# Attention earlier in a unit, k and v of two heads in one transfer, and part of the q loads on SyncE's queue

## The chip, the cores and the metric

The kernel runs on one core of one Trainium2 chip. The metric is the device time in microseconds (us) of one execution, the median over several runs. TensorE multiplies matrices, VectorE and ScalarE do element-wise work, and three queues issue the DMA transfers: those of SyncE (SP in the profile), of GpSimd (POOL) and, at the start and the end, of ScalarE (ACT).

## The reference

Linear attention per head, a normalisation, and then a feed-forward layer with a squared ReLU:

```python
# q, k, v: (8 batches, 8 heads, 576 positions, 64)   all fp32
kv  = np.einsum('bhsd,bhse->bhde', k, v)         # one 64x64 matrix per batch and head
out = np.einsum('bhsd,bhde->bhse', q, kv)
rms = np.sqrt(np.mean(out * out, axis=-1, keepdims=True) + 1e-06)
x   = (out / rms * g_norm)                       # then (b,h,s,d) -> (b*s, h*d) = (4608, 512)
h = x @ w_in                                     # (4608, 2048)
r = np.maximum(h, 0.0)
g = s * (r * r) + b
y = g @ w_out                                    # (4608, 512)
```

## The kernel before

The 4608 rows are cut into nine units (u = 0 to 8) of 512 rows. A unit's first product (x @ w_in) has four steps, s = 0 to 3, and each step seven partial products (x1, z2, x6, y7, x5, x3, y4) of a Strassen-like scheme, so that VectorE and ScalarE add pieces between them. A unit's second product (g @ w_out) has the same seven partial products, and in units 2 to 8 the scheme is applied twice. While TensorE works on unit u, the attention for unit u + 1 is computed in two pairs of 128-row chunks, A and B, whose steps are hung into slots between the partial products.

Each engine works through its instructions in the order in which the program lists them, so the slot decides what stands ahead of what. The slots of the first product:

```python
        for s in range(NS if u > 0 else 0):
            a = steps[s]
            at(0)                       # runs first[(s, 0)]
            a["x1"]()
            if s:
                x3(steps[s - 1])        # product 3 of the step before, and its VectorE work
            a["z2"]()
            at(1)
            if s:
                y4(steps[s - 1])
            a["x6"]()
            at(2)
            a["y7"]()
            if s == NS - 1 and u > 1:
                second["sums"]()        # four sums for the second product
            at(3)
            a["x5"]()
```

What fills them, in unit 2 and in units 3 to 7:

```python
        kv = [lambda: kv_product(kv_due[u]), lambda: pump(NP)] if u in kv_due else []
        q = {half: [partial(loads, u + 2, half)] for half in range(2)}
        ...
        if u == 2:
            first = {
                (0, 2): [A["turn"]],
                (1, 1): kv,
                (1, 3): [A["product"]],
                (2, 0): [A["back"]],
                (2, 1): [A["square"]],
                (2, 2): [A["row_sum"], B["turn"]],
                (2, 3): [B["product"]],
                (3, 0): [B["back"]],
                (3, 1): [A["norm"]],
                (3, 2): [A["turn_x"], *q[0]],
                (3, 3): [B["square"]],
            }
            second = {
                0: [A["scale"]], 3: [B["row_sum"]], "norm": [B["norm"]],
                4: [B["turn_x"], B["scale"], *q[1]],
            }
        else:
            first = {
                (0, 2): [A["turn"]],
                (0, 3): [A["product"]],
                (1, 0): [A["back"]],
                (1, 1): [A["square"], *kv],
                (1, 2): [A["row_sum"]],
                (1, 3): [B["turn"]],
                (2, 0): [A["norm"]],
                (2, 1): [B["product"], *q[0]],
                (2, 2): [A["turn_x"], B["back"]],
                (2, 3): [B["square"]],
                (3, 0): [A["scale"], B["row_sum"]],
                (3, 1): [B["norm"]],
                (3, 2): [B["turn_x"], *q[1]],
            }
            second = {0: [B["scale"]]}
```

The steps: `turn` transposes q (VectorE), `product` multiplies it by kv (TensorE), `back` transposes the result (VectorE), `square` and `scale` are ScalarE's, `row_sum`, `norm` and `turn_x` VectorE's.

The loads. k and v of a batch come in four pairs of heads, one pair to a tile of a ring of seven, which the pieces of w_out share. `pump(k)` issues the next k ring loads on SyncE:

```python
    def load_kv_into(t, b, n):
        kv_in[b, n] = t.rearrange("p (m j d) -> p m j d", m=2, j=R)
        for m, src in enumerate((k, v)):
            for r in range(2):
                nc.sync.dma_start(
                    out=kv_in[b, n][r * HB : r * HB + HB, m],      # 64 partitions
                    in_=src[b, NP * r + n].rearrange("(p j) d -> p j d", j=R),
                )
```

q of a pair of chunks comes in 16 or 32 small loads on GpSimd (`load_q`, where `rest` is issued by `nc.gpsimd.dma_start`). In unit 1 the second product has 14 slots, numbered 0 to 13; `pump(2)` stands in the slots 1, 3, ... 13, and these are hung in after a slot's own work:

```python
                5: [A["row_sum"], B["turn"]],
                6: [A["norm"], partial(loads, 3, 0)],     # q of unit 3, first pair
                7: [A["turn_x"], A["scale"], B["product"], B["back"], B["square"]],
                8: [B["row_sum"]],
                9: [B["norm"], partial(loads, 3, 1)],     # q of unit 3, second pair
                11: [B["turn_x"], B["scale"]],
                12: [sums],
```

In unit 1 the pieces of w_out for the twice-applied scheme are also made, by VectorE, and stored to DRAM by GpSimd, once each for the products 1, 2, 6, 7, 3 and 4. A ring tile that holds such a piece is free only when its store has landed:

```python
        def parts_of_w(i):
            y = [[ring[u, i, n][:, :, q * P : q * P + P] for q in range(2)] for n in range(2)]
            (y11, y12), (y21, y22) = y
            ...                                           # t1 .. t4: four subtractions on VectorE
            for n, t in enumerate((y11, y21, t2, t3, t1, y22, t4)):
                nc.gpsimd.dma_start(out=w3_dram[i][:, n], in_=t)
```

The product of k and v works on 64x64 tiles of the array; r is the row half (one head each), l the head pair, and before the change l is also the column half:

```python
                for l in range(2):
                    for r in range(2):
                        rows = slice(r * HB, r * HB + HB)
                        nc.tensor.matmul(
                            ps[r][l * HB : l * HB + HB, i, :],
                            lhsT=kv[l][rows, 0, j, :],
                            rhs=kv[l][rows, 1, j, :],
                            start=(j == 0), stop=(j == R - 1),
                        )
```

Of the kernel before, what the change touches and what calls it, by code (L numbers as in the profile page):

```python
# [16 lines left out]
def kernel(  # L17
# [39 lines left out]
    nc = tc.nc  # L57
    P = 128
    B, H, S, D = q.shape
# [33 lines left out]

    kv_in, q_in, q_tile, w_raw = {}, {}, {}, {}

    def load_kv(b, i, pool, queues=(nc.sync, nc.sync), **kw):

        t = pool.tile([P, 4 * R * D], U32, name="kv_sb", **kw)
        view = t.bitcast(FP32).rearrange("p (m l j d) -> p m l j d", m=2, l=2, j=R)
        for l in range(2):  # L100
            kv_in[b, 2 * i + l] = view[:, :, l]
        for m, src in enumerate((k, v)):
            for r, queue in enumerate(queues):
                h = NP * r + 2 * i
                queue.dma_start(
                    out=view[r * HB : r * HB + HB, m].rearrange("p l j d -> p l (j d)"),
                    in_=src[b, h : h + 2].rearrange("h (p j) d -> p h (j d)", j=R),
                )

    def load_kv_into(t, b, n):  # L110

        kv_in[b, n] = t.rearrange("p (m j d) -> p m j d", m=2, j=R)
        for m, src in enumerate((k, v)):
            for r in range(2):
                nc.sync.dma_start(
                    out=kv_in[b, n][r * HB : r * HB + HB, m],
                    in_=src[b, NP * r + n].rearrange("(p j) d -> p j d", j=R),
                )

    def parts(c):  # L120

# [7 lines left out]
            return [(2 * g, 16, 2), (2 * g + 1, 0, 2)]  # L129
        return [(2 * g, 4 * i, 4)] if i < 4 else [(2 * g + 1, 4 * i - 18, 4)]  # L130

    def load_q(c, queues=(nc.sync, nc.sync)):

        t = qp.tile([P, 2 * DM], FP32, name="q_sb", tag="q")
        q_tile[c] = t
        pieces = []
        for i in range(2):
            if c + i < R:  # L140
                q_in[c + i] = t[:, i * DM : i * DM + DM].rearrange("p (h d) -> p h d", h=H)
        for s, queue in enumerate(queues):
            for i in range(2):
                if c + i < R:
                    b, j, _ = parts(c + i)[s]
                    queue.dma_start(
                        out=q_in[c + i][s * HB : s * HB + HB],
                        in_=q[b].rearrange("h (p j) d -> p j h d", j=R)[:, j],
                    )
        for i in range(2):  # L150
            if c + i < R:
                continue
            w = 4 * i
            for b, j, n in parts(c + i):
                if pieces and pieces[-1][1] == b and pieces[-1][2] + pieces[-1][3] == j:
                    pieces[-1][3] += n
                else:
                    pieces.append([w, b, j, n])
                w += n
            q_in[c + i] = t.rearrange("p (a w) -> p a w", a=NP)[:, :, i * P : i * P + P]  # L160
            if c + i == R:
                q_in[R] = t[:, DM:].rearrange("p (a w) -> p a w", a=NP)
        rest = []
        for w, b, j, n in pieces:
            src = q[b].rearrange("h (t j) d -> h t j d", j=JC)
            to = t.rearrange("p (a w d) -> p a w d", a=NP, d=32)
            if c < R:
                to, w = t[:, DM:].rearrange("p (a w d) -> p a w d", a=NP, d=32), 0
            for h in range(H):
                for a in range(2):  # L170
                    rows = slice(32 * (2 * (h % 2) + a), 32 * (2 * (h % 2) + a) + 32)
                    rest.append(
                        partial(
                            nc.gpsimd.dma_start,
                            out=to[rows, h // 2, w : w + n, :],
                            in_=src[h, :, j : j + n, a * 32 : a * 32 + 32],
                        )
                    )
        return rest
# [189 lines left out]
    def kv_product(b):  # L369


        ps = [ps_t.tile([P, 2, D], FP32, name="kv_ps", tag="t") for _ in range(2)]
        for i in range(2):
            if b == 0:
                warm((18, 7)[i])
            kv = [kv_in.pop((b, 2 * i + l)) for l in range(2)]
            for j in range(R):
                for l in range(2):
                    for r in range(2):
                        rows = slice(r * HB, r * HB + HB)  # L380
                        nc.tensor.matmul(
                            ps[r][l * HB : l * HB + HB, i, :],
                            lhsT=kv[l][rows, 0, j, :],
                            rhs=kv[l][rows, 1, j, :],
                            start=(j == 0),
                            stop=(j == R - 1),
                        )
        for r in range(2):
            for l in range(2):
                ls = slice(l * HB, l * HB + HB)  # L390
                to = bd_kv[b % 2][ls, 2 * r : 2 * r + 2, ls].rearrange("p i (c e) -> p i c e", c=KC)
                src = ps[r][ls].rearrange("p i (e c) -> p i c e", c=KC)
                if b == 0 and l == 1:
                    nc.vector.tensor_copy(out=to, in_=src)
                else:
                    nc.scalar.copy(to, src)
# [915 lines left out]
    def side_of(u):  # L1312

        A, B = pairs_of(u + 1)
        sums = lambda: [fn() for fn in x_sums(u + 1)]
        if u == 0:
            side = {
                6: [lambda: kv_product(1)],
                7: [partial(A["turn"], 0), partial(A["turn"], 1)],
                8: [A["product"], A["back"], A["square"]],  # L1320
                9: [A["row_sum"], partial(B["turn"], 0), partial(B["turn"], 1)],
                10: [A["norm"], A["turn_x"], A["scale"], B["product"], B["back"], B["square"]],
                11: [B["row_sum"], B["norm"]],
                12: [B["turn_x"], B["scale"], lambda: [fn() for fn in sums_w_in(0)]],
                13: [sums],
            }
        else:
            side = {
                2: [partial(A["turn"], 0), partial(A["turn"], 1)],
                4: [A["product"], A["back"], A["square"]],  # L1330
                5: [A["row_sum"], B["turn"]],
                6: [A["norm"], partial(loads, 3, 0)],
                7: [A["turn_x"], A["scale"], B["product"], B["back"], B["square"]],
                8: [B["row_sum"]],
                9: [B["norm"], partial(loads, 3, 1)],
                11: [B["turn_x"], B["scale"]],
                12: [sums],
            }
        return side

    def loads(u, i):

        if u < U:
            for load in load_q(4 * u + 2 * i):
                load()  # L1345

    tile_at = {1: 3, 2: 4, 3: 5, 4: 6, 5: 7, 6: 8, 7: 9, 9: 10, 10: 11, 11: 12, 12: 13, 14: 14, 15: 15}
    more_at = {8: 8, 9: 9, 12: 10, 13: 11, 14: 12, 15: 13}
# [19 lines left out]
    def sides(u):  # L1368
# [15 lines left out]
# [5 lines that stand above are left out]
                (2, 0): [A["back"]],  # L1389
                (2, 1): [A["square"]],  # L1390
                (2, 2): [A["row_sum"], B["turn"]],
                (2, 3): [B["product"]],
                (3, 0): [B["back"]],
                (3, 1): [A["norm"]],
                (3, 2): [A["turn_x"], *q[0]],
                (3, 3): [B["square"]],
            }
            second = {
                0: [A["scale"]], 3: [B["row_sum"]], "norm": [B["norm"]],
                4: [B["turn_x"], B["scale"], *q[1]],  # L1400
            }
        else:
            first = {
                (0, 2): [A["turn"]],
                (0, 3): [A["product"]],
                (1, 0): [A["back"]],
                (1, 1): [A["square"], *kv],
                (1, 2): [A["row_sum"]],
                (1, 3): [B["turn"]],
                (2, 0): [A["norm"]],  # L1410
                (2, 1): [B["product"], *q[0]],
                (2, 2): [A["turn_x"], B["back"]],
                (2, 3): [B["square"]],
                (3, 0): [A["scale"], B["row_sum"]],
                (3, 1): [B["norm"]],
                (3, 2): [B["turn_x"], *q[1]],
            }
            second = {0: [B["scale"]]}
        second[5], second[6] = [[lambda n=n: x_sums(u + 1)[n]()] for n in range(2)]
        return first, second  # L1420

# [92 lines left out]
```

## Time and profile before

The time before is 949.64 us, the median of 3 runs (949.62 to 950.98).

| engine | busy us | share of the span of 948.0 us | instructions |
|---|---|---|---|
| TensorE, matmul | 920.6 | 97% | 7118 |
| TensorE, weight load | 828.4 | 87% | 7118 |
| VectorE | 668.6 | 71% | 1175 |
| ScalarE | 197.6 | 21% | 355 |
| GpSimd | 249.2 | 26% | 458 |

The units in the trace of TensorE: unit 1 ends at 241.4 us, unit 2 runs to 354.7, unit 3 to 454.1, and each later unit takes about as long. A group "x8" of a matmul with fp32 operands is four matmuls: each leaves two records. The list of waits names who waited, for whom, the microseconds in total, the number of times and the longest. The timeline gives a start, a duration, the engine, the line, and how many instructions were merged; in brackets stands the idle time before it and what ended it. "SPq" and "POOL" lines with DMA_DIRECT2D are issues of transfers, not the transfers themselves.

### The profile page before, as it was taken

How to read it: one execution, taken by the hardware profiler on the slowest of the kernel's cores; microseconds unless marked ns; L12 is line 12 of the kernel's file. 1: busy time of each engine (PE TensorE's matmuls, PEld its weight loads, DVE VectorE, ACT ScalarE, POOL GpSimd, SP SyncE). 2: the span in 40 equal slices, each digit the busy share in tenths (PEclk: the TensorE clock that was granted, in tenths of full speed). 3: DMA queues.
4: the chain of work that ended last, by engine and by line, in shares of the span. 5: the costliest groups of instructions: out<-in, count | busy, mean ns of one | idle time of the engine just before them, and what ended most of it. 6: DMA issues, size and time to landing. Idle time of an engine off the chain costs nothing. (4 is left out here: it accounts for less than half of the span.)

```text
span 948.0 us, 17626 instructions
## 1 busy us (share of the span) xinstructions
PE 920.6 (97%) x7118; PEld 828.4 (87%) x7118; DVE 668.6 (71%) x1175; ACT 197.6 (21%) x355; POOL 249.2 (26%) x458
## 2 busy tenths in 40 slices
PE   8999999999889999999999999999999999999997
PEld 7888888888767998889888988899889988998997
DVE  2789777587527785787568766776778767774585
ACT  3683132101112102220232012300231023101200
POOL 2000017056921132370337033613250200021000
PEclk9999999999979999999999999999999999999999
DMA  9688839279480686158624773278217810681065
GB/s 261 201 285 248 271 95 258 59 236 298 112 287 15 209 261 217 23 149 273 213 69 120 244 237 96 68 247 284 96 42 226 292 31 12 202 289 54 12 232 168
DMA packets 78624, 165.80 MB, mean 175 GB/s; under 512 B 22608, under 2 KB 31824, under 8 KB 78416
## 3 DMA queue, kind: packets, MB, share of 16 engines
q1 hardware_dynamic: 58096, 135.62, 44.9%
q0 software_dynamic: 16704, 26.51, 9.8%
q10 hardware_dynamic: 3744, 2.56, 1.1%
q8 instruction: 56, 0.92, 0.4%
q14 instruction: 24, 0.20, 0.1%
HBM read 136.84 MB, written 27.79 MB: 174 GB/s over the span
## 5 line engine op out<-in xcount | busy, mean ns | idle before, releaser
L1345 POOL DMA_DIRECT2D q_sb<-in_q_dram x288 | 161.2, 568 | 204.2 <-issue 111.8
L920 POOL DMA_DIRECT2D out_dram<-o x110 | 54.7, 504 | 361.2 <-DVE o L251 214.4
L694 ACT COPY r<-x_ps 128x512 f32<-128x512 f32 x96 | 56.1, 584 | 442.3 <-PE x_ps L91 399.8
L91 PE MATMUL y_ps<-xs,wb 128*128 128x256 f32 x512 | 123.8, 385 | 3.2 <-DVE a L251 3.2
L251 DVE TENSOR_TENSOR a<-y_ps,r 128x512 f32<-128x512 f32 x64 | 44.0, 688 | 115.1 <-ACT r L694 80.6
L91 PE MATMUL x_ps<-xs,ws 128*128 128x256 f32 x512 | 122.5, 382 | 2.3 <-ACT r L694 2.3
L91 PEld LDWEIGHTS x_ps<-xs,ws 128*128 128x128 f32 x512 | 96.0, 190 | 20.1 <-ACT r L694 4.7
L91 PEld LDWEIGHTS y_ps<-xs,wb 128*128 128x128 f32 x512 | 96.7, 192 | 18.8 <-DVE a L251 4.3
L91 PE MATMUL x_ps<-xT,wa 128*128 128x256 f32 x384 | 89.6, 380 | 0.1
L91 PEld LDWEIGHTS x_ps<-xT,wa 128*128 128x128 f32 x384 | 72.3, 190 | 10.2 <-ACT xT L501 0.5
L91 PE MATMUL y_ps<-w_sb,sub 128*128 128x128 f32 x560 | 69.5, 275 | 0.6 <-DVE sub L254 0.6
L91 PEld LDWEIGHTS y_ps<-w_sb,sub 128*128 128x128 f32 x560 | 66.4, 192 | 1.2 <-DVE sub L254 0.8
L649 DVE SCALAR_TENSOR_TENSOR a<-a 128x512 f32<-128x512 f32 x89 | 61.5, 691 | 2.8
L91 PE MATMUL y_ps<-w_sb,a 128*128 128x128 f32 (+1 forms) x416 | 61.0, 295 | 0.0
L91 PE MATMUL x_ps<-xT,ws 128*128 128x256 f32 x256 | 60.5, 379 | 0.0
L91 PE MATMUL z_ps<-xT,wa 128*128 128x256 f32 x256 | 60.5, 379 | 0.0
L91 PE MATMUL x_ps<-w_sb,s 128*128 128x256 f32 x256 | 57.8, 380 | 0.0
L91 PEld LDWEIGHTS y_ps<-w_sb,a 128*128 128x128 f32 x416 | 55.5, 192 | 2.0
L91 PE MATMUL t_ps<-w_sb,sub 128*128 128x128 f32 x448 | 54.9, 275 | 0.5 <-DVE r L816 0.5
L91 PEld LDWEIGHTS z_ps<-xT,wa 128*128 128x128 f32 x256 | 48.6, 190 | 6.6
L91 PEld LDWEIGHTS x_ps<-xT,ws 128*128 128x128 f32 x256 | 48.1, 190 | 6.3
L91 PEld LDWEIGHTS t_ps<-w_sb,sub 128*128 128x128 f32 x448 | 52.3, 192 | 0.8 <-DVE r L816 0.7
(160 smaller groups left out, 1402.6 us busy)
## 6 DMA issues: line engine op xcount, KB each, us to landing
w_sb<-w SPq DMA_DIRECT2D x154, 512.0 KB, 4.9
w_sb<-w SPq DMA_DIRECT2D x42, 256.0 KB, 3.9
w_raw<-in_moe_w_in_dram SPq DMA_DIRECT2D x8, 1024.0 KB, 7.6
w_raw<-in_moe_w_out_dram SPq DMA_DIRECT2D x8, 1024.0 KB, 5.2
w_sb<-in_k_dram SPq DMA_DIRECT2D x48, 144.0 KB, 4.3
w_sb<-in_v_dram SPq DMA_DIRECT2D x48, 144.0 KB, 4.4
w<-sub POOLq DMA_DIRECT2D x24, 256.0 KB, 5.4
out_dram<-o POOLq DMA_DIRECT2D x92, 64.0 KB, 4.9
```

The lines of the kernel that those rows point to most:

```text
L91: nc.tensor.matmul(o, lhsT=lhsT, rhs=rhs, start=start, stop=stop, skip_group_check=True)
L251: nc.vector.tensor_tensor(out=o, in0=a, in1=b, op=ALU.add)
L649: nc.vector.scalar_tensor_tensor(t, t, 0.0, t, ALU.max, ALU.mult)
L694: nc.scalar.copy(st[name], src)
L920: queues[s % 2].dma_start(out=view[b, jj, :, cols], in_=st[name, j][s * w : s * w + w, cols])
L1345: load()
```

## The change

Three things are changed. First, the steps of the attention of the next unit start with the first slot of a unit's first product (units 3 to 7) or are moved up by a slot or so (unit 2). They are to keep clear of the last step and of the second product. Second, k and v of two neighbouring heads, which lie together in DRAM, come in one transfer over 128 partitions in place of two over 64. The heads are thereby numbered otherwise, and the product's result is placed in column half `r ^ l` and copied across partition halves where needed. Third, in unit 1 the q loads of unit 3's first pair go on SyncE in eight parts, and those of the second pair are issued on GpSimd after the last slot, so that GpSimd's queue is clear for the stores of w_out's pieces.

```diff
     def load_kv_into(t, b, n):
         kv_in[b, n] = t.rearrange("p (m j d) -> p m j d", m=2, j=R)
         for m, src in enumerate((k, v)):
-            for r in range(2):
-                nc.sync.dma_start(
-                    out=kv_in[b, n][r * HB : r * HB + HB, m],
-                    in_=src[b, NP * r + n].rearrange("(p j) d -> p j d", j=R),
-                )
+            nc.sync.dma_start(
+                out=kv_in[b, n][:, m],
+                in_=src[b, 2 * n : 2 * n + 2].rearrange("r (p j) d -> (r p) j d", j=R),
+            )
 ...  (load_kv for batches 0 and 1 in the same manner; load_q gets a parameter rest_on)
-                            ps[r][l * HB : l * HB + HB, i, :],
+                            ps[r][(r ^ l) * HB : (r ^ l) * HB + HB, i, :],
 ...
         for r in range(2):
+            rs = slice(r * HB, r * HB + HB)
             for l in range(2):
-                ls = slice(l * HB, l * HB + HB)
-                to = bd_kv[b % 2][ls, 2 * r : 2 * r + 2, ls].rearrange("p i (c e) -> p i c e", c=KC)
-                src = ps[r][ls].rearrange("p i (e c) -> p i c e", c=KC)
+                cs = slice((r ^ l) * HB, (r ^ l) * HB + HB)
+                to = bd_kv[b % 2][rs, l:NP:2, rs].rearrange("p i (c e) -> p i c e", c=KC)
+                src = ps[r][cs].rearrange("p i (e c) -> p i c e", c=KC)
 ...  (unit 1, second product)
-                6: [A["norm"], partial(loads, 3, 0)],
+                6: [A["norm"]],
                 7: [A["turn_x"], A["scale"], B["product"], B["back"], B["square"]],
                 8: [B["row_sum"]],
-                9: [B["norm"], partial(loads, 3, 1)],
+                9: [B["norm"]],
                 11: [B["turn_x"], B["scale"]],
                 12: [sums],
+                13: [partial(loads, 3, 1)],
             }
+            for n, fn in enumerate(loads_in_parts(3, 0, 8)):      # eight parts, rest_on=nc.sync
+                side.setdefault(6 + n, []).append(fn)
 ...  (unit 2)
-                (2, 3): [B["product"]],
-                (3, 0): [B["back"]],
-                (3, 1): [A["norm"]],
-                (3, 2): [A["turn_x"], *q[0]],
-                (3, 3): [B["square"]],
+                (2, 3): [A["norm"], B["product"]],
+                (3, 0): [A["turn_x"], *q[0]],
+                (3, 1): [A["scale"]],
+                (3, 2): [B["back"]],
             }
             second = {
-                0: [A["scale"]], 3: [B["row_sum"]], "norm": [B["norm"]],
-                4: [B["turn_x"], B["scale"], *q[1]],
+                0: [B["square"]], 2: [B["row_sum"]], "sums": [B["norm"]],
+                "norm": [B["turn_x"]], 4: [B["scale"], *q[1]],
             }
 ...  (units 3 to 7: the list shown above is replaced by)
+                (0, 0): [A["turn"]],
+                (0, 1): [A["product"]],
+                (0, 2): [A["back"]],
+                (0, 3): [A["square"], B["turn"]],
+                (1, 0): [A["row_sum"]],
+                (1, 1): kv,
+                (1, 2): [A["norm"], A["turn_x"]],
+                (1, 3): [B["product"], *q[0]],
+                (2, 0): [B["back"], A["scale"]],
+                (2, 1): [B["square"]],
+                (2, 2): [B["row_sum"]],
+                (2, 3): [B["norm"]],
+                (3, 0): [B["turn_x"], *q[1]],
+                (3, 1): [B["scale"]],
```

## The prediction

> **What bounds the kernel now.** I read the page first, then TensorE's list of waits, then its timeline in the stretch that holds the longest wait, then the queues of GpSimd and SyncE there, and last VectorE and ScalarE around the small waits.
>
> ```profile
> PE 920.6 (97%) x7118; PEld 828.4 (87%) x7118; DVE 668.6 (71%) x1175; ACT 197.6 (21%) x355; POOL 249.2 (26%) x458
> PEclk9999999999979999999999999999999999999999
> ...
> PE kv_ps L381 <- DMA w_sb<-in_v_dram: 8.7, 2, 8.1
> PE y_ps L91 <- DVE a L251: 3.2, 6, 0.5
> PE x_ps L91 <- ACT r L694: 2.3, 5, 0.5
> ```
>
> TensorE is busy 97% of the span, so the time is TensorE's work plus its waits, and no matmul of the large products is removed by the change. What can be won is the list of waits (us in total, times, longest). One is large: the k-by-v product of one batch waits 8.7 us for v. The clock row shows one slice of 40 with a lower granted clock, the one with that wait. The rest is many waits of about half a microsecond.
>
> ```profile
> 253.51 1.89 PE L91 MATMUL z_ps<-xT,wa 128*128 128x256 f32 x8
> 255.33 1.38 PE L381 MATMUL kv_ps<-w_sb 64*64 64x64 f32 x76
> 264.80 0.44 PE L381 MATMUL kv_ps<-w_sb 64*64 64x64 f32 x2 [8.09 <-DMA w_sb<-in_v_dram]
> 265.86 2.15 PE L381 MATMUL kv_ps<-w_sb 64*64 64x64 f32 x66 [0.62 <-DMA w_sb<-in_v_dram]
> 267.94 3.15 PE L91 MATMUL y_ps<-xs,wb 128*128 128x256 f32 x8
> 270.93 1.89 PE L91 MATMUL x_ps<-xs,ws 128*128 128x256 f32 x8
> ```
>
> This is unit 2 (start us, us, records). From 255.33, where the product starts, to 270.93, where the second matmul group after it starts, are 15.6 us. The same stretch of unit 3 runs from 369.81 (product, x144) by 372.30 (y_ps) to 374.13 (x_ps): 4.32 us. The wait therefore costs 11.3 us, not 8.7: after it, 66 records take 2.15 us (33 ns each, against 18 ns for 144 in 2.56 us in unit 3), and the next group 3.0 us instead of 1.73.
>
> Why is v late? The queues of GpSimd and of SyncE:
>
> ```profile
> 228.87 10.39 POOL L1345 DMA_DIRECT2D q_sb<-in_q_dram  x19 [0.86 <-DMA w<-sub]
> 240.22 12.38 POOL L1345 DMA_DIRECT2D q_sb<-in_q_dram  x22 [0.96 <-DMA q_sb<-in_q_dram]
> 252.59 1.08 POOL L920 DMA_DIRECT2D out_dram<-o  x2
> 253.67 1.55 POOL L832 DMA_DIRECT2D w<-w_sb  x2
> ...
> 233.60 1.23 SPq L115 DMA_DIRECT2D w_sb<-in_v_dram  x2
> 256.74 1.10 SPq L115 DMA_DIRECT2D w_sb<-in_k_dram  x2
> 257.88 3.29 SPq L115 DMA_DIRECT2D w_sb<-in_v_dram  x2
> ...
> SPq L115 <- DMA w<-w_sb: 21.8, 1, 21.8
> ```
>
> The last of four k/v pairs goes into a ring tile that still holds a piece of w_out which GpSimd has to store to DRAM first (line 832). VectorE's sums for that store begin at 231.67, but its DMA is issued only at 253.67: 48 loads of q at about 0.57 us each stand ahead of it in GpSimd's queue from 222.83 to 252.6. SyncE waits 21.8 us for that store and issues the pair at 256.74, after TensorE has come to the product.
>
> The small waits lie in the last step (s = 3) of the first product in units 3 to 7:
>
> ```profile
> 403.61 1.99 PE L91 MATMUL x_ps<-xs,ws 128*128 128x256 f32 x8 [0.47 <-ACT r L694]
> 407.92 1.99 PE L91 MATMUL y_ps<-xs,wb 128*128 128x256 f32 x8 [0.53 <-DVE a L251]
> 401.06 1.22 DVE L583 TENSOR_TENSOR xn<-q_sb,inv 128x1024 f32<-128x1024 f32 x1
> 402.20 0.68 DVE L251 TENSOR_TENSOR a<-y_ps,r 128x512 f32<-128x512 f32 x1
> ```
>
> ScalarE's copy r (402.98) waits for the buffer that the add at 402.20 frees, and that add stands behind the normalisation of the second attention pair (0.25 + 1.22 us). Then transpose (1.24 us at 403.53) and four sums delay the next add to 407.19, the second wait. It is 0.47 + 0.53 = 1.0 us a unit.
>
> **What the Trainium skill says.** "DMA: Bandwidth & Descriptors", section "Anatomy of one DMA — SWDGE (gpsimd) path": a semaphore wait is taken on the issuing sequencer before dispatch, so what stands behind a waiting or slow transfer in the same queue stands too. The trace agrees: 21.8 us of SyncE's queue behind one store. "TensorE: Matmul & The Clock Gate", section "Part 1: The HAM clock gate": after an idle window of about 3.4 us the array falls to half rate until it has been busy for such a window. The trace agrees: 33 ns against 18 ns a record after 8.09 us idle, and the granted clock of the stretch 241.4 to 304.2 is 0.92 where its neighbours have 1.00. "TensorEngine Tiling (Array Packing)", section "Key Properties": different tiles work in parallel. The k-by-v records last 218 ns and start 18 ns apart, so they overlap here; whether the new order of tiles overlaps more, no trace yet shows.
>
> **The change part by part.**
>
> (a) Loads of q for unit 3. The 32 loads of the first pair leave GpSimd's queue for SyncE's, in eight groups of four through the slots 6 to 13 of unit 1's second product; the 16 of the second pair stay on GpSimd but come after the last store. The stores of line 832 for product 3 then start when their sums and the output ahead of them are ready: output at 231.75, two DMAs of 0.5 us, so 232.8 instead of 253.67, 20.9 us earlier. The last k/v pair, 3.1 us behind that store before (253.67 to 256.74), is issued near 236 and lands about 4.4 us later, near 241. TensorE needs it at 255.3: the wait goes, with the slow clock after it. Gain 11.3 us.
>
> (b) What SyncE now has ahead of its own loads. In the new order its last four q loads stand behind two ring loads that need the stores for product 4. In the old trace the y22 store, the last but one of these 14 stores, was issued at 265.12, 11.45 us after the first (253.67). Shifted to 232.8 it goes at 244.3. SyncE's first ring load of that kind (262.72) came 5.9 us after its store (256.82); so the ring is free at 250.2. One ring load (some 0.4 us) and four q loads (I take 0.6 us each from the 64-row k loads, 1.14 us for two) end at 253.0; with 2.1 to 3 us of landing the q tile is whole at 255 to 256. VectorE wants to transpose it at 246.49 and takes its work in order, so it stands 9 us. What must follow is 1.24 us of transpose and 0.69 us of add before TensorE's y_ps group, which without the old wait comes at 255.3 + 2.5 = 257.8. Limit for the q tile: 255.9. Most of the 9 us is thus hidden; I charge 0.8 us, with up to 4 if the stores land slowly.
>
> (c) Attention one or two slots earlier in units 3 to 7. Same instructions; the transposes of q go into s = 0, where VectorE has no adds of an earlier step, and norm and transpose of the second pair leave the slots ahead of the add of s = 3. Removed there: 0.25 + 1.22 us ahead of the first add, 2.7 us ahead of the second, against waits of 0.47 and 0.53. Five units by 1.0 us are 5.0. The first pair's product now comes right after z2 of s = 0: in unit 3 VectorE ends its last sum at 356.66, transposes to 357.9, TensorE arrives at 358.14, so there is 0.2 us to spare. I take 4.5 us for small remains.
>
> (d) Unit 2. Norm and transpose of A leave s = 3 for s = 2; B's transpose back (1.3 us) comes there instead of 2.7 us, so its wait of 0.54 us goes. In its second product B's row sum (1.21 us) leaves the crowded stretch 340 to 351, where 0.46 and 0.62 us are waited; I take half of that. The 1.0 us at 289.01 stays, as transpose and product of B keep their slots. Sum 1.0 us.
>
> (e) k/v in one transfer of 288 KB for two of 144 KB: eight fewer SyncE issues a batch at 0.6 us each, none ahead of a waiting engine except in (a); nothing. The product's tiles now alternate both halves. Per batch it is 2.56 us of TensorE, eight batches 20.5 us; I take 3% of this, 0.6 us, as it may bring nothing.
>
> Sum: -11.3 + 0.8 - 4.5 - 1.0 - 0.6 = -16.6; 949.6 - 16.6 = 933.0 us, or 1.7% less.
>
> **The rivals.** First: the wait changes its place. SyncE's queue holds q, k/v and weights in one order, and if the stores for product 4 land at 256 rather than 250, the q tile comes at 261, TensorE stands 5 us and may cool again. For it: those stores' landing is the least certain term (ring loads at 219.96 and 227.31 came about 8 us after their stores). Against: 9 us of VectorE's stand are covered. Time: 937 to 940. Second: the new tile order of the k-by-v product overlaps better. Before, two neighbours in the order share the array's column half; after, neighbours share neither rows nor columns. If that took 4 ns of the 18 ns a record, 1152 records would give 4.6 us: 929, below the 2% line of 930.7. For it: the layout of the data did not ask for this order of tiles. Against: records of 218 ns that start 18 ns apart overlap twelvefold already. Third: VectorE gets a new knot at s = 0 or in the second product of unit 2, half a microsecond in each of six units: 936.
>
> **Range and chances.** The sure part is (a): 10 to 11.3 us. Small waits give 3.5 to 6, the rivals -4 to +5. So 928.5 to 938.5 for 8 in 10. Beyond 2% needs the small terms whole and some of the second rival: 0.2. Slower by 2% would need a new wait of over 30 us: 0.01.
>
> **What would show it.** Right: no wait of kv_ps for in_v_dram in unit 2; the first w<-w_sb store of product 3 near 233; the granted clock at 9 in every slice; the 0.5 us waits at s = 3 gone. (b) shows as the start of the transpose of q in unit 2 (near 255) and a wait of y_ps for VectorE there. Wrong: a wait of over 3 us there, the k-by-v product not at 2.56 us, or new waits of the first pair's product for qT.

## The result and the profile after

| | median us | lowest to highest | runs |
|---|---|---|---|
| before, beside it | 950.31 | 949.62 to 956.6 | 4 |
| after | 939.97 | 938.83 to 940.94 | 4 |

The ratio is 0.9876, with a 95% interval of 0.9833 to 0.992. The prediction was 933.0 us with a range of 928.5 to 938.5: the time fell, but by some 10 us and not by 17.

From the page of the changed kernel, its rows of busy time and of granted clock, and then its list of TensorE's waits (us in total, times, longest):

```profile
PE 917.5 (98%) x7118; PEld 828.2 (88%) x7118; DVE 670.3 (72%) x1175; ACT 196.5 (21%) x355; POOL 232.4 (25%) x426
PEclk9999999999989999999999999999999999999999
```

```profile
PE y_ps L91 <- DVE a L251: 4.9, 1, 4.9
PE xT_ps L485 <- ACT w_raw L231: 2.0, 1, 2.0
...
PE y_ps L551 <- DVE inv L582: 1.0, 1, 1.0
...
PE t_ps L91 <- DVE sub L254: 0.7, 1, 0.7
```

The wait for v (8.7 us) has gone, and so have the ten small waits at s = 3. In their place stands one wait of y_ps for VectorE, and the clock still has one slice below 9. Unit 2 in TensorE's timeline shows where:

```profile
255.77 1.89 PE L91 MATMUL z_ps<-xT,wa 128*128 128x256 f32 x8
257.59 2.37 PE L381 MATMUL kv_ps<-w_sb 64*64 64x64 f32 x144
264.84 3.78 PE L91 MATMUL y_ps<-xs,wb 128*128 128x256 f32 x8 [4.87 <-DVE a L251]
268.41 2.73 PE L91 MATMUL x_ps<-xs,ws 128*128 128x256 f32 x8
270.98 1.89 PE L91 MATMUL y_ps<-xs,wb 128*128 128x256 f32 x8
272.80 1.26 PE L551 MATMUL y_ps<-qT,bd_kv 64*32 64x192 f32 x64
```

The k-by-v product now runs through. The next group waits 4.87 us, and after that a group takes 3.57 us to the next one's start, then 2.57, where 1.83 and 1.73 are usual behind this product. The granted clock was 0.50 from 264.8 to 268.4 us and 0.67 from there to 271.0. VectorE's timeline and SyncE's queue give the reason:

```profile
262.96 1.25 DVE L530 STREAM_TRANSPOSE qT<-q_sb 128x1024 f32<-128x1024 f32 x1 [14.14 <-DMA w_sb<-w]
264.13 0.65 DVE L251 TENSOR_TENSOR a<-y_ps,r 128x512 f32<-128x512 f32 x1
```

```profile
254.39 1.09 SPq L786 DMA_DIRECT2D w_sb<-w  x2
255.52 1.84 SPq L1360 DMA_DIRECT2D q_sb<-in_q_dram  x4
```

VectorE stands 14.14 us ahead of the transposition of unit 3's q, and the add that TensorE needs stands behind it. The releaser named, w_sb, landed just before; what the transposition reads is q_sb. The last four q loads were issued at 255.5 to 257.0, right behind two ring loads. The summary of these four (duration of an issue in ns: shortest, median, longest; then us from issue to landing) and that of the eight loads of the two parts before:

```profile
L1360 SPq DMA_DIRECT2D q_sb<-in_q_dram x4: 368/426/430, 255.5 to 257.0; - x4
...
DMA to landing us min/median/max: 5.7/5.9/6.2
```

```profile
L1360 SPq DMA_DIRECT2D q_sb<-in_q_dram x8: 504/1067/1483, 245.8 to 253.5; - x8
...
DMA to landing us min/median/max: 4.3/5.9/7.5
```

So q was whole at 262.7 (257.0 + 5.7).

Unit by unit, from one start of a unit's first product to the next (us). "After, again" is the same kernel profiled once more (the fourth experiment):

| | first large product | unit 1 | unit 2 | unit 3 | unit 4 | unit 5 | unit 6 |
|---|---|---|---|---|---|---|---|
| before | 25.30 | 102.56 | 113.25 | 99.44 | 99.59 | 99.50 | 99.63 |
| after | 28.59 | 102.35 | 108.28 | 97.69 | 97.85 | 97.77 | 97.86 |
| after, again | 25.39 | 102.34 | 110.75 | 97.69 | 97.86 | 97.76 | 97.86 |

### The profile page after: what moved, and what is told of

Read it like the earlier page. It is cut to its first block, busy times and chain, and to the rows that moved or that the text cites. A ratio compares the mean times of both kernels' runs of the same rounds, so it can differ in the third digit from the quotient of the medians.

```text
span 937.0 us, 17537 instructions
## 1 busy us (share of the span) xinstructions
PE 917.5 (98%) x7118; PEld 828.2 (88%) x7118; DVE 670.3 (72%) x1175; ACT 196.5 (21%) x355; POOL 232.4 (25%) x426
## 4 chain that ended last, share of the span: by engine, by line
PE 93%; DVE 3%; DMA 2%; ACT 1%; issue 0%; SPq 0%; DVEq 0%; ACTq 0%
PE x_ps L91 42%; PE y_ps L91 29%; PE z_ps L91 10%; PE t_ps L91 8%; PE y_ps L551 2%; PE kv_ps L381 2%; DMA w_raw<-in_moe_w_in_dram 1%; DMA kv_sb<-in_k_dram 1%; DMA w_sb<-w 0%; DVE sub L254 0%; DVE qT L530 0%; DVE ss L574 0%; PE qT_ps L540 0%; ACT w_raw L231 0%; DVE a L251 0%
## 5 line engine op out<-in xcount | busy, mean ns | idle before, releaser
L1349 POOL DMA_DIRECT2D q_sb<-in_q_dram x256 | 144.1, 571 | 159.3 <-issue 123.7
```

## The experiments

**1. Five parts in place of eight.** The q loads end with slot 10, ahead of the ring loads that wait for product 4's pieces.

```diff
-            for n, fn in enumerate(loads_in_parts(3, 0, 8)):
+            for n, fn in enumerate(loads_in_parts(3, 0, 5)):
```

> The changed kernel, but unit 3's 32 loads of q go on SyncE in five parts (slots 6 to 10) in place of eight, so that none stands behind a ring load that waits for a store. Theory A (order of the queue: the last q loads stood behind the ring loads that wait for the stores of product 4, and behind their 1 MB on the same queue): the transpose of q in unit 2 starts before 250, TensorE's 4.9 us wait and the slow clock after it go, the time falls by 6.5 to 8 us against the changed kernel, to about 932.5. Theory B (the DMA engines as a whole are saturated there, whatever the order): q lands no earlier than 258, or k and v come as late instead, and the time stays within 2 us of 940.

930.32 us (928.52 to 931.33); ratio to before 0.9791 [0.9771, 0.981]. Unit 2 takes 101.24 us. VectorE and TensorE in its trace:

```profile
253.64 1.25 DVE L530 STREAM_TRANSPOSE qT<-q_sb 128x1024 f32<-128x1024 f32 x1 [8.06 <-DMA w_sb<-in_k_dram]
254.81 0.65 DVE L251 TENSOR_TENSOR a<-y_ps,r 128x512 f32<-128x512 f32 x1
```

```profile
254.34 1.38 PE L381 MATMUL kv_ps<-w_sb 64*64 64x64 f32 x76
255.93 1.26 PE L381 MATMUL kv_ps<-w_sb 64*64 64x64 f32 x68 [0.21 <-DMA w_sb<-in_v_dram]
257.12 1.99 PE L91 MATMUL y_ps<-xs,wb 128*128 128x256 f32 x8
```

The transposition begins 13.2 us after the start of the unit (253.64 - 240.43) and not 19.3 (262.96 - 243.69), later than the 250 that theory A expected. VectorE still stands 8.06 us, and none of it reaches TensorE: the add is done at 255.5, before the next group starts at 257.12. So unit 2's excess goes with the late q: 108.28 - 101.24 = 7.0 us in the first trace of the changed kernel, 9.5 in the second. The slow q loads now stand ahead of the last k/v pair, and v comes 0.21 us late: the product takes 2.78 us to the next start, 0.5 more than in the changed kernel.

**2. Units 3 to 7 with their old slots**, all else as changed (the list of the kernel before in place of the new one).

> The changed kernel with the attention slots of units 3 to 7 as before. Theory A (the earlier slots take away the two waits of 0.5 us at s = 3 and their restarts, the rest of the units' gain is the k-by-v product): the two waits come back, each unit gets 1.2 to 1.5 us longer, the time rises by 6 to 7.5 us. Theory B (most of the gain in these units comes from elsewhere, the tile order or the transfers): it rises by less than 4 us.

943.33 us (942.9 to 944.23); ratio 0.9931 [0.9914, 0.9947]. The two waits a unit are back:

```profile
396.91 1.99 PE L91 MATMUL x_ps<-xs,ws 128*128 128x256 f32 x8 [0.46 <-ACT r L695]
...
401.22 1.99 PE L91 MATMUL y_ps<-xs,wb 128*128 128x256 f32 x8 [0.54 <-DVE a L251]
```

Units 3 to 6 take 99.22 to 99.41 us. Laid beside the repeat of the changed kernel (experiment 4) group by group, the groups on either side of the first wait take 0.73 us more from start to start and those on either side of the second 0.80: 1.53 a unit, 7.7 us in five. The medians differ by 5.1 (943.33 - 938.25), as unit 2 was 2.6 us shorter in this run (108.16 against 110.75).

**3. The column half of the k-by-v product by head pair again.**

```diff
-                            ps[r][(r ^ l) * HB : (r ^ l) * HB + HB, i, :],
+                            ps[r][l * HB : l * HB + HB, i, :],
```

> The changed kernel with the column half l in place of r xor l in the product of k and v; transfers and slots as changed. Theory A (neighbours in the order that share neither rows nor columns overlap better): the product of 144 records takes 2.49 us from its start to the next group's instead of 2.27, and the time rises by 1 to 1.8 us. Theory B (the shorter product comes from the operands' arrival or the layout of the transfers): it stays at 2.27 and the time stays within 0.5 us.

937.71 us (936.89 to 940.01); ratio 0.9874 [0.9853, 0.9895].

```profile
366.67 2.34 PE L381 MATMUL kv_ps<-w_sb 64*64 64x64 f32 x144
368.94 1.99 PE L91 MATMUL y_ps<-xs,wb 128*128 128x256 f32 x8
```

The product takes 2.27 us to the next start, as with the new order (367.10 to 369.37 in the changed kernel) and less than the 2.49 of before. The order of the tiles brings nothing.

**4. The changed kernel once more**, with no edit, on the chip of experiments 1 to 3.

> The changed kernel itself once more, for its spread. Theory A (the 3 us that its first trace lost before the first large product came from the start's transfers and differ from run to run): this trace starts its first large product at another time than 28.6 us, between 25 and 29. Theory B (the new order of heads in the first k and v loads costs the 3 us): again 28 to 29 us.

938.25 us (936.17 to 939.33); ratio 0.9874 [0.985, 0.9899]. The first large product begins at 25.39, so the 3.3 us of the first trace's start are no property of the change. But y_ps waits 7.6 us here for 4.9: q is whole at 262.0 here and at 262.7 in the first trace, though unit 2 began 3.5 us earlier.

**5. q of the first pair on GpSimd again, only the second pair moved behind the last slot.**

```diff
-                6: [A["norm"]],
+                6: [A["norm"], partial(loads, 3, 0)],
...
-            for n, fn in enumerate(loads_in_parts(3, 0, 8)):
-                side.setdefault(6 + n, []).append(fn)
```

> The changed kernel, but unit 3's first pair of q stays on GpSimd at slot 6 as before; only the second pair comes after slot 13. Theory A (it is enough that 16 of the 48 loads no longer stand ahead of the stores; SyncE isn't needed): GpSimd's 32 loads end near 242, the first store of product 3 goes near 244, the last k and v are there by 254, q long before; TensorE waits 2 us at most in unit 2, the time is 931 to 934. Theory B (any q on GpSimd at slot 6 holds the stores back too long): the product of k and v waits 4 us or more for v and the array slows, 937 or more.

931.07 us (929.78 to 934.84); ratio 0.9819 [0.9788, 0.985]; unit 2 takes 102.33 us. The first store of product 3 goes at 244.67, the last k/v pair at 247.71, and the k-by-v product waits for nothing. The 16 loads of the second pair, 9 us of GpSimd's queue, were enough to make v late; the 32 of the first pair need not leave. What is paid is a wait of 2.5 us for the second pair's attention (1.0 in the changed kernel):

```profile
PE y_ps L551 <- DVE inv L582: 2.5, 1, 2.5
```

**6. Seven parts**, so that the last part stands ahead of the last two ring loads (`loads_in_parts(3, 0, 7)`; one run).

> The changed kernel with seven parts (slots 6 to 12): the last q loads stand behind the ring load of slot 11, but ahead of the two of slot 13. Theory A (the two ring loads of slot 13 make q late, by their wait for the stores of product 4 and by 1 MB on the same queue): the transpose of q in unit 2 starts near 252 to 256 instead of 263, TensorE's wait for it is under 2 us. Theory B (the DMA engines are saturated, order does not matter): the wait stays over 4 us.

934.54 us; unit 2 takes 105.46 us, y_ps waits 2.9. The wait lies between the two expectations. The q loads end at 256.4, hardly earlier than with eight parts, but the last two land 3.3 to 3.4 us after issue and not 5.9: without the two ring loads directly ahead of them. Unit 2 is 2.8 and 5.3 us shorter than in the two traces of eight parts and 4.2 us longer than with five: the two ring loads are a good part of the delay. That the slow issues ahead of them are the rest is likely, but no run takes them away alone.

**7. Only the tail of the second pair at its old slots** in units 3 to 7: norm, transpose and scale (one run).

```diff
-                (2, 3): [B["norm"]],
-                (3, 0): [B["turn_x"], *q[1]],
-                (3, 1): [B["scale"]],
+                (3, 1): [B["norm"]],
+                (3, 2): [B["turn_x"], *q[1]],
             }
+            second = {0: [B["scale"]]}
```

> The changed kernel, but in units 3 to 7 the last steps of pair B alone come as late as before (norm at (3,1), transpose at (3,2), scale at slot 0 of the second product). Theory A (the two waits at s = 3 come from these two VectorE steps ahead of its adds, not from where the attention begins): both waits are back, a unit takes 1.4 to 1.6 us longer than in the changed kernel (99.2 for 97.7). Theory B (the gain comes from the early start): a unit takes at most 0.5 us longer.

942.56 us. Units 3 to 6 take 98.74 to 98.91 us, 1.05 more than in the changed kernel, of the 1.53 of experiment 2 and between the two expectations. The second wait is back (0.53), the first is only a gap of 0.14 us. So with the rest early, moving these three steps back takes away two thirds of the gain.

**8. k and v in two transfers of 64 partitions again**, with the new heads and tiles.

```diff
-            nc.sync.dma_start(
-                out=kv_in[b, n][:, m],
-                in_=src[b, 2 * n : 2 * n + 2].rearrange("r (p j) d -> (r p) j d", j=R),
-            )
+            for r in range(2):
+                nc.sync.dma_start(
+                    out=kv_in[b, n][r * HB : r * HB + HB, m],
+                    in_=src[b, 2 * n + r].rearrange("(p j) d -> p j d", j=R),
+                )
```

> The changed kernel with the ring loads of k and v as two transfers of 64 partitions each, same heads and same tiles. Theory A (each of 16 waits for a landed transfer costs the product some 25 to 30 ns, and the change leaves 8): the 144 records of units 3 to 6 take 2.49 us to the next group's start, instead of 2.27. Theory B (the heads' new order or the start of the operands makes it shorter): 2.27 as in the changed kernel.

943.02 us (one run). Unit 2 takes 113.25 us, as y_ps waits 10.3: SyncE has more issues ahead of q. The k-by-v product of units 3 to 6 takes 2.63, 2.54, 2.49 and 2.49 us to the next start, against 2.27 in the changed kernel and 2.49 before.

**9 and 10. Five parts and two slots of unit 2 changed; beside it five parts alone.** The turn of the second pair's q moves from slot (2, 2) to (2, 1), its norm from the four sums to the slot behind the first group of the second product.

```diff
-                (2, 1): [A["square"]],
-                (2, 2): [A["row_sum"], B["turn"]],
+                (2, 1): [A["square"], B["turn"]],
+                (2, 2): [A["row_sum"]],
...
-                0: [B["square"]], 2: [B["row_sum"]], "sums": [B["norm"]],
+                0: [B["square"]], 2: [B["row_sum"]], ("q", 0): [B["norm"]],
```

> q of unit 3 in five parts on SyncE, as in the first experiment, and unit 2's slots changed in two places: the turn of q of the second pair moves from behind the row sum of the first to the slot before it, and its normalisation moves out of the four sums for the second product to the slot behind the first group of that product. Theory A: the two waits left in unit 2 of the first experiment (1.0 us of y_ps at the inverse, 0.7 of t_ps at VectorE, each with about 0.26 us that the list doesn't show) go, unit 2 falls from 101.24 us to 98.9 to 99.7, and the time is 1.5 to 2.5 us under that of the five parts alone, 928 to 929. Theory B: VectorE is so full in that stretch that the waits only change their place: unit 2 stays at 100.5 to 101.5, the time within 0.7 us of the five parts alone.

> The kernel of the first experiment once more, on the chip of the run beside it: 930 to 931 us, unit 2 at 101.2 us, no wait of y_ps for VectorE's add behind the transposition of q. If the start of the program alone moves (first large product between 25.2 and 28.6), the unit lengths stay within 0.1 us and the time moves by as much as the start.

The ninth: 928.32 us (927.31 to 929.18), ratio 0.9757 [0.9731, 0.9783]. The tenth: 930.18 us (928.85 to 934.27), ratio 0.9782 [0.9754, 0.981]. The intervals overlap. In the traces the wait of y_ps at the inverse has gone (the group ahead of it takes 1.82 us and not 2.87), but one of the two waits of t_ps stands a group later with the same cost in sum (0.30 and 0.54 us for 0.68 and 0.16), and v came 0.75 us late:

```profile
256.79 1.26 PE L381 MATMUL kv_ps<-w_sb 64*64 64x64 f32 x68 [0.75 <-DMA w_sb<-in_v_dram]
```

From the start of unit 2 to that of unit 8 it is 587.10 us against 587.25. So of two waits one went, one changed its place, and most of that gain was lost to v. Both kernels beat the changed one and the one before; which of the two is faster stays open.

**11. The last three of eight parts on ScalarE's queue**, where no other transfer stands.

```diff
             for load in left[:k]:
-                load()
+                nc.scalar.dma_start(**load.keywords) if n > 4 else load()
```

> The changed kernel, but the last three of the eight parts of q (12 loads, slots 11 to 13 of unit 1) are issued by ScalarE's queue, which holds no other transfer there; the ring loads stay on SyncE. Theory A (q is late because of its place in SyncE's queue): ScalarE issues them by about 242, they land by 250, the transposition of q in unit 2 starts before 252, y_ps does not wait for VectorE, unit 2 falls from 108 to 110.8 us to 100.8 to 102, and the time to 929 to 931. Theory B (the DMA engines are full in that stretch, whatever the queue): the 12 loads land no earlier than 258, y_ps still waits over 3 us and unit 2 stays above 106.

941.08 us (940.15 to 941.84); ratio 0.9906 [0.989, 0.9923]. Both theories missed: the loads made a wait of their own. TensorE's and ScalarE's timelines:

```profile
255.47 3.78 PE L91 MATMUL x_ps<-xs,ws 128*128 128x256 f32 x8 [10.53 <-ACT r L695]
```

```profile
242.91 11.88 ACTq L1360 DMA_DIRECT2D q_sb<-in_q_dram  x12
254.83 0.59 ACT L695 COPY r<-x_ps 128x512 f32<-128x512 f32 x1 [16.84 <-DMA q_sb<-in_q_dram]
```

Twelve issues hold ScalarE for 11.88 us, and its copy r, which TensorE needs, stands behind them. The issues are as slow on this queue (up to 1.97 us for one) as on SyncE's, though no ring load stands in it. The last of them, issued from 252.4 on, take 0.44 us and land 3.5 to 4.2 us later, less than the 5.9 behind the ring loads; SyncE issued no ring load between 245.31 and 255.48 here.

**12. The kernel of 8 with the column half by head pair as well** (one run).

> The kernel with the loads split into two of 64 partitions, and now also with the column half of the k-by-v product by head pair as before the change. Theory A (the order of the tiles matters where each product waits for twice as many transfers): the product of units 3 to 6 takes 2.49 us to the next group's start as before the change, not 2.63. Theory B (the order of the tiles brings nothing with these waits either): 2.6 to 2.65, and what makes 2.49 of it before the change is something else. The time stays at 942 to 944 in either case, as the wait for q in unit 2 stays.

942.95 us. The product of units 3 to 6 takes 2.63, 2.55, 2.49 and 2.48 us, the same as in experiment 8 to 0.01. With twice as many transfers the order of the tiles brings nothing either; the number of transfers makes 2.49 of 2.27. What adds another 0.14 in unit 3 and 0.05 in unit 4 stays open.

**13. Half of each store for the products 3 and 4 at its time**, the other half of its place filled earlier from other pieces. This kernel leaves out the right second halves of w_out's pieces for these two products. It stores the other halves with the products 1 and 2; the order of the rest stays.

```diff
-                nc.gpsimd.dma_start(out=w3_dram[i][:, n], in_=t)
+                half = FC // 8 if i in (3, 4) else FC // 4
+                nc.gpsimd.dma_start(out=w3_dram[i][:, n, :half], in_=t[:, :half])
+                if i < 3:
+                    nc.gpsimd.dma_start(out=w3_dram[i + 2][:, n, FC // 8 :], in_=t[:, FC // 8 :])
```

> The changed kernel, but of each piece of w_out for the products 3 and 4 only the first half is stored at its time (128 KB for 256); the other half of its place in DRAM is filled 35 to 45 us earlier, from the pieces of the products 1 and 2. So the products 3 and 4 of the twice-applied scheme compute with other numbers, while every transfer, its order and every wait stay; 1.8 MB less move between 232 and 250. Theory A (full DMA engines stretch the issues of the q loads, 1.07 us each for 0.44, and their landing, 5.9 us): the eight loads ahead of the last ring loads take under 5.5 us, all land before 256, y_ps waits under 1 us (4.9 and 7.6 before), unit 2 falls to 101 to 103 us, the time to 930 to 932. Theory B (only the place behind the ring loads in SyncE's queue makes q late): the issues still take about 1 us each, the transposition of q in unit 2 starts after 259 and unit 2 stays above 106.

936.48 us (one run). SyncE's queue (lines stand three further down in this kernel) and TensorE's timeline:

```profile
247.75 5.84 SPq L1363 DMA_DIRECT2D q_sb<-in_q_dram  x8
253.75 0.86 SPq L786 DMA_DIRECT2D w_sb<-w  x2
254.65 1.84 SPq L1363 DMA_DIRECT2D q_sb<-in_q_dram  x4
```

```profile
263.45 3.61 PE L91 MATMUL y_ps<-xs,wb 128*128 128x256 f32 x8 [6.09 <-DVE a L251]
```

The eight loads take 5.84 us, not 8.43, and one issue 0.31 to 0.50 us, though 2.1 us of the 5.84 are a wait for a transfer in flight (last section); this fits stores that slow the issues. But the eight loads before them took 8.95 us here and 5.94 in the changed kernel, the ring loads still go at 253.75, the last q loads land at 259.5 to 261.3, the transposition starts at 261.58 and unit 2 takes 108.49 us. Lighter stores alone do not bring q in time behind the ring loads; with q ahead of them (experiment 1) it is.

## Why the prediction was wrong, step by step

**(a) q off GpSimd's queue: right.** Predicted was a first store of product 3 at 232.8; it came at 235.38 in a run that started 2.3 us later. No wait for v is left in unit 2, and with q in time (experiment 1) unit 2 is 12.0 us shorter than before, against 11.3 + 1.0 predicted for (a) and (d) together, although v was a little late there. But only the second pair had to leave its place (experiment 5).

**(b) what stands ahead of the last q loads: this step failed.** The term was 0.8 us, "with up to 4 if the stores land slowly"; the runs give 7.0 and 9.5 (unit 2 of the changed kernel less unit 2 of experiment 1). As v cost experiment 1 itself 0.5 us, the late q alone costs 7.6 and 10.0: from the k-by-v product to the small product behind it (L551) there are 15.21 us in the first trace (257.59 to 272.80) and 17.67 in the second, where 2.27 + 1.83 + 1.73 + 1.82 = 7.65 are usual. The chain was the right one, and four of its terms were too small. All predicted times are shifted here by the later start of 2.3 us:

| | predicted | measured |
|---|---|---|
| last but one store of product 4 landed | 252.5 | 255.0 |
| ring loads begin | 252.5 | 254.4 |
| q loads issued | 255.3 | 257.4 |
| q tile whole | 257.3 to 258.3 | 262.7 |
| latest for y_ps | 258.2 | |

First and second, the ring loads were held by a store and by the q loads ahead of them, and the two overlap. The last but one store of product 4 (y22), on GpSimd:

```profile
L833 POOL DMA_DIRECT2D w<-w_sb x1: 760/760/760, 247.7 to 247.7; - x1
...
DMA to landing us min/median/max: 7.4/7.4/7.4
```

It landed at 255.0, and the second ring load waited its last 0.3 us for it. The prediction had taken 5.9 us from the store of product 3 in the old trace; that of product 4 took 9.3 there. The eight q loads ahead of the ring loads held SyncE's queue from 245.8 to 254.2, with a median of 1.07 us each; at the 0.6 us that the prediction took for such a load they would have ended by 250.6. By these figures either alone would have put the last q loads at 255 or later (an estimate). In the second trace the store landed at 252.2 and the ring loads went at 253.9 and 254.4, so there it was the q loads.

Third, landing: "2.1 to 3 us" were 5.7 to 6.2. Issue and landing (issue plus the us to landing of each) in SyncE's queue:

| issued | what | landed, after | issued | landed, experiment 13 |
|---|---|---|---|---|
| 254.4 | ring load | 258.5 | 253.7 | 257.3 |
| 255.1 | ring load, 512 KB | 261.4 | 254.3 | 258.9 |
| 255.5 | q, 8 KB | 261.7 | 254.7 | 259.5 |
| 257.0 | q, 8 KB | 262.7 | 256.1 | 261.3 |

In these traces a small load landed only after the large ones that were issued ahead of it. This is where "DMA: Bandwidth & Descriptors" of the Trainium skill, section "Queues, rings and completion order", should have been read with the queue's list: on each DMA engine the descriptors of a queue are taken in ring order, and the increment of a semaphore lands only after every earlier write of that engine. The traces agree: in both columns the landings keep the order of issue, and in experiment 6, where no ring load is directly ahead of the last two, their landing takes 3.3 to 3.4 us. The page adds that the transfers of one issuing engine need not complete in order; in these two stretches they did.

Fourth, the cost of the wait: 4.87 us listed are 7.6 us of time, as the first two groups after it take 3.57 and 2.57 us for 1.83 and 1.73. "TensorE: Matmul & The Clock Gate", section "Part 1: The HAM clock gate", has a window of about 3.4 us without work before the rate falls. The wait of 4.87 us agrees; but the slow groups follow the wait of 2.9 us in experiment 6 too (3.19 and 2.05 us to the next start, granted clock 0.56 from 261.5 to 264.6), so here less was enough, while after 2.5 us in experiment 5 no group was slow (clock 1.00).

The first rival, that the wait changes its place, is what happened: q at 261, TensorE standing 5 us and cooling, 937 to 940 us. Its ground, stores that land late, was a part of it: in the first trace they were 2.5 us late and not 6, and the slow q loads held the queue nearly as long.

**(c) earlier slots in units 3 to 7: right in kind, too small.** Predicted 4.5, measured 7.7. Each unit was taken for the sum of its two listed waits, 1.0; it is 1.53. A listed wait of 0.47 or 0.53 us costs 0.73 or 0.80, as the first group after a wait takes 1.83 us for 1.73, and the one ahead of it runs out for 0.16 us past the time at which its successor would have started.

**(d) unit 2: the sum was right, by luck.** From the second group behind the k-by-v product to the end of the unit there are 83.75 us before (270.93 to 354.68) and 82.72 in experiment 1 (258.95 to 341.67): 1.0 less, as predicted. But all of it lies at s = 3, where the wait of 0.54 us and the gaps beside it were worth 1.0 and not 0.5: from the y_ps group at 300.51 to the group behind the one that waited (308.52) there were 8.01 us, and 6.97 in the changed kernel (298.82 to 305.79). From there to the end of the unit it is 46.16 us before and 46.18 after, so the second product gained nothing of the 0.5: waits of t_ps of 0.18, 0.68 and 0.16 us stand where 0.46 and 0.62 stood. The 1.0 us wait of the second pair's product stayed, as said.

**(e) k/v: the gain came from the part that was charged nothing.** Predicted 0.6 for the tiles, nothing for the transfers. The product fell from 2.49 to 2.27 us, 1.3 us in the six batches that come through the ring, by the transfers (experiments 8 and 12), none of it by the tiles (3 and 12). The second rival is out. And "none ahead of a waiting engine" did not hold once q shared the queue: with two transfers again (experiment 8) y_ps waits 10.3 us.

In sum: with 7.6 and 10.0 in place of 0.8 for (b), -7.7 for (c), -1.0 for (d) and -1.3 for (e) the sum is -13.7 for the first trace and -11.3 for the second. The profiled spans went from 948.0 to 937.0, with a start of unit 1 that was 2.5 us later, and to 936.0, with one that was 1.0 us earlier; without the starts that is -13.5 and -11.0.

## What to carry to other kernels

When a load is moved to another queue, write down everything that stands ahead of it there, with bytes, and take its landing as that of the last large transfer ahead of it; here four loads of 8 KB behind a megabyte landed just after it. Moving work off a queue also moves the transfers that it held back, here into the very stretch in which the moved loads were issued. A wait in the list is a lower bound of what it costs: here a half-microsecond one cost half as much again, and a 5 us one cost 7.6.

## What the runs showed that was not expected

**An issue of a small load is not of one length.** Loads of one form took 0.44 us of SyncE at 228.6 to 232.8 (median) and 1.07 at 245.8 to 253.5, while the stores of w_out's pieces were in flight; the DMA engines were as full at 228 to 231 (378 GB/s, against 367 at 245 to 254). That it goes with the stores fits experiments 11 and 13, but is not shown; by what mechanism stays open.

**SyncE seems to keep eight transfers in flight.** In experiment 13 four q loads were issued at 242.5, 244.2, 245.9 and 253.3, each in the tenth of a microsecond in which the eighth transfer before it landed, and SyncE's list of waits there names it:

```profile
SPq L1363 <- DMA w_sb<-in_v_dram: 2.5, 2, 1.4
SPq L1363 <- DMA w_sb<-w: 2.1, 1, 2.1
SPq L1363 <- DMA w_sb<-in_k_dram: 1.3, 1, 1.3
```

**More transfers make the product that reads them slower**, though the trace lists no wait for them in units 3 to 6: 2.49 against 2.27 us for 144 records, with two transfers in place of one for each of k and v of a pair.

**The start of the program varies**: the first large product began at 28.59 and at 25.39 us in two traces of the changed kernel.
